# An attention and channel-mix kernel: loads of S and k spread over two DMA queues, output stored by 32-partition groups, fewer products on a zeroed tile

## The chip, the cores and the metric

The kernel runs on one core of one Trainium2 chip. A core has five engines that run their own instruction streams and meet at semaphores: PE (TensorE: products, with the weight loads listed apart as PEld), DVE (VectorE), ACT (ScalarE), POOL (GpSimd) and SP (SyncE). SP and ACT also issue DMAs; each has a queue of its own in the profile, SPq and ACTq. The metric is device microseconds of one execution.

## The reference

Two stages. The first is linear attention with a feature map that multiplies two sketches of a vector by each other; the second is a channel mix with a token shift.

```python
# q, k, v: (4 batches, 4 heads, 1088 tokens, 32), S1, S2: (8, 32)
def phi(x):
    a = einsum('rd,bhsd->bhsr', S1, x)
    b = einsum('rd,bhsd->bhsr', S2, x)
    return einsum('bhsi,bhsj->bhsij', a, b).reshape(..., 64)
q_p, k_p = phi(q), phi(k)
kv = einsum('bhsf,bhsd->bhfd', k_p, v)
z = sum(k_p, axis=2)
x = (q_p @ kv) / (q_p @ z + 1e-6)          # then heads side by side: (4, 1088, 128)

x_prev = x shifted by one token (a zero first)
xk = mu_k * x + (1 - mu_k) * x_prev
xr = mu_r * x + (1 - mu_r) * x_prev
out = sigmoid(xr @ w_r) * (relu(xk @ w_k) ** 2 @ w_v)     # w_k: 128 x 1024, w_v: 1024 x 128
```

## The kernel before

A batch has 1088 tokens, held as 34 blocks of 32: partition p of a tile stands for one of 32 token groups (of one head, or of all), and the 34 places within a group lie along the row. Each batch goes through three stages.

`stage_k` (from line 288) transposes k in two halves (kT, L296), multiplies by the masked sketch `Skb` (L303), transposes the result back (abT, L310), forms the 64 features (phk, L317) and accumulates kv with v (L326). The result `w` is masked on DVE (L336) and copied by two DMAs with its partition halves swapped (`ws`, L337).

`stage_q` transposes q (qT, L350), expands the features with `WS` (L362, copies on ACT at L374, products on DVE at L379), multiplies by w (L393) and divides by the denominator (L410 to L445). Its result is xT.

`stage_m` does the channel mix in three chunks of token blocks, `CH`: 12, 12 and 10 blocks of 32 tokens. Of a chunk it forms xk (L469), multiplies by w_k in eight products (L490), applies relu (kr, L495 on ACT or L497 on DVE), squares (the tile k2, named k in the profile: L499 on DVE or L501 on ACT), multiplies by w_v (L519), and by w_r for the gate (L514, sigmoid sg at L526); DVE forms the output tile `o` (L528), which has 128 tokens-of-a-product as partitions and three products side by side. SP stores o (L532). A product covers four blocks of 32 tokens; `first` names the column at which each of the three products begins. In a chunk of 10 blocks the third begins at column 192, so it overlaps the second, and only two of its blocks are stored. Store number i writes m blocks of product i, with a pattern whose outer count is m (4, or 2), then 32 token groups, then 128 values of four bytes; the rows in memory are 512 bytes long.

The order of the work on all engines is written out by hand: every operation has a number, and the string `ORDER` (L85 to L123) names them one after the other; "*5" behind a number puts five products on a zeroed tile (`stir`, L538, recorded as L540) ahead of it. Each engine works strictly through its own part of this order. The operation numbered 0 is the first `stir`, with 24 products. Ahead of it stand the loads that are issued in the code's own order: S1 and S2 on ACT's queue (L169, L170; both go into the tile Sst, which DVE transposes into St at L234, and from which Skb and WS come), then the two halves of the first k and the four parts of the first v on SP's (L181, L189), and the first q on ACT's (L202). All other loads are in `ORDER`, on SP. The chunks of the four batches are interleaved in it, so the last chunks to be computed are not the last in the code.

A DMA signals its completion on one of eight semaphores, taken in turn by all DMAs of both queues; in the orders below they read DMAHW0 to DMAHW7. A DMA waits, where its row says so, for the one before it on the same semaphore.

Of the kernel before, what the change touches and what calls it, by code (L numbers as in the profile page):

```python
# [17 lines left out]
def _ap(ap, new_ap, off=0):  # L18
    return dataclasses.replace(ap, ap=new_ap, offset=ap.offset + off)
# [13 lines left out]
class _Plan:  # L33
# [7 lines left out]
    def op(self, eng, cost, name, fn, need=(), uses=(), mode=None, kb=None, after=0.0, alt=(), stir=None):  # L41
        need = [n for n in need if n is not None]
        after = max([after] + [n["at"] for n in need if "at" in n])
        o = {"ways": [(eng, cost, fn)] + list(alt), "name": name, "need": [n for n in need if "at" not in n],
             "uses": list(uses), "mode": mode, "kb": kb, "after": after, "n": len(self.ops), "stir": stir}
        self.ops.append(o)
        return o
# [18 lines left out]
def kernel(  # L66
# [14 lines left out]
    nc = tc.nc  # L81
    B, H, S, D = q.shape
    R = S1.shape[0]
    DM, FF = moe_w_k.shape
    P = 128  # L85
    NFF = FF // P
    NB = S // 32
# [52 lines left out]
    op = plan.op  # L140

    def sb(tag, shape, dtype=F32, bufs=2):
        return _Buf(work, tag, bufs, shape, dtype)
# [3 lines left out]
    def ps(shape=(P, 512)):  # L147

        pair = shape[1:] == [KP, 512] and KP == 2
        t = _Buf(psum, None, 1, list(shape), F32)  # L150
        t.kind = "pair" if pair else "bank"
        banks.append(t)
        return t

    def dve(n, rate=0.96e3):
        return n / rate + 0.067
# [8 lines left out]
    Sst = const.tile([P, 2, D], F32)  # L165
    idle = const.tile([P, 512], BF16)
    nc.vector.memset(idle[:], 0.0)  # L167
    rows = [[D, R], [1, D]]
    nc.scalar.dma_start(Sst[:, 0, :], _ap(S1, [[0, 16]] + rows))  # L169
    nc.scalar.dma_start(Sst[:, 1, :], _ap(S2, [[0, 16]] + rows))  # L170

    kin = [const.tile([P, NB, D], F32, name=f"kin{b}") for b in range(3)]
# [2 lines left out]
    qTs = [const.tile([P, NB, 32], F32, name=f"qT{i}") for i in range(2)]  # L175
    LKB = NB * D * P * 4 / 1024

    def load_k(b, cuts):
        src = k[b].rearrange("h (sp t) d -> (h sp) t d", sp=32)
        for lo, hi in zip(cuts, cuts[1:]):  # L180
            nc.sync.dma_start(kin[b % 3][:, lo:hi, :], src[:, lo:hi, :])  # L181

    def load_q(b):
        nc.sync.dma_start(qin[b % 3][:], q[b].rearrange("h (sp t) d -> (h sp) t d", sp=32))
# [11 lines left out]
    wk = const.tile([DM, FF], BF16)  # L196
    wv = const.tile([P, NFF, DM], BF16)

    load_k(0, [0, NB // 2, NB])
    for g in range(4):  # L200
        load_v(0, g, nc.sync)
    nc.scalar.dma_start(qin[0][:], q[0].rearrange("h (sp t) d -> (h sp) t d", sp=32))  # L202
# [14 lines left out]
    for u in range(2):  # L217
        for p in range(2):
            lo = 32 + R * (2 * p + u)
# [36 lines left out]
    def arrival(nm, b):  # L256
        if (nm, b) not in IN:
            t = ARRIVE[nm][b]
            need = done[nm, b - 3] if b > 2 else []
            if nm == "k":  # L260
                IN[nm, b] = op("SP", 0.55, f"k{b}", lambda: load_k(b, [0, NB]), need, kb=LKB, after=t)
            elif nm == "q":
                IN[nm, b] = op("SP", 0.55, f"q{b}", lambda: load_q(b), need, kb=LKB, after=t)
            else:
                IN[nm, b] = [op("SP", 0.6, f"v{b}", lambda g=g: load_v(b, g, nc.sync), need, kb=LKB / 4, after=t)
                             for g in range(4)]
        return IN[nm, b] if isinstance(IN[nm, b], list) else [IN[nm, b]]
# [188 lines left out]
    def stage_m(b, xT, xo):  # L456
# [5 lines left out]
        order = (1, 2, 0)  # L462
        for j, ci in enumerate(order):
            c0, n = CH[ci]
# [7 lines left out]
            lo, hi = (0, 13) if ci == 0 else (c0 + 1, c0 + n + 1)  # L472
# [5 lines left out]
        for j, ci in enumerate(order):  # L478
            c0, n = CH[ci]
            k2 = sb("k2", [P, NFF, 12 * 32], BF16, 3)  # L480
            ok = []
            for cc in range(NFF // 2):
                kr = sb("kr", [P, 2, 12 * 32], BF16, 6)
                o2 = []
                for i0 in range(0, 2, KP):
                    kp = ps([P, KP, 512])

                    def up(kp=kp, c=2 * cc + i0, c0=c0, n=n):
                        for i in range(KP):
# [4 lines left out]
                            stir=lambda n, kp=kp: stir(kp[:, 0, :], n))  # L494
# [10 lines left out]
            o = sb("o", [P, 3, P], F32, 4)  # L505
            nt = (n + 3) // 4

            first = [128 * i if 4 * i + 4 <= n else 32 * n - P for i in range(nt)]

            def gate(rg=rg, c0=c0, first=first):  # L510
                for i, t in enumerate(first):
# [5 lines left out]
            def down(i, rd=rd, k2=k2, first=first):  # L517
                for c in range(NFF):
# [4 lines left out]
                    stir=lambda n, rg=rg: stir(rg.t.rearrange("p i m -> p (i m)"), n))  # L523
# [3 lines left out]
                sg[:, :nt, :], rg[:, :nt, :], ACTF.Sigmoid), [og], [rg, sg])  # L527
            oo = [op("DVE", dve(nt * P), f"o{b}.{ci}", lambda nt=nt, rd=rd, sg=sg, o=o: nc.vector.tensor_mul(  # L528
                o[:, :nt, :], rd[:, :nt, :], sg[:, :nt, :]), [os_] + od, [rd, sg, o])]
            def store(i, m, c0=c0, o=o, first=first):  # L530
                t = c0 + first[i] // 32 + 4 - m
                nc.sync.dma_start(_ap(out[b], [[DM, m], [NB * DM, 32], [1, DM]], t * DM), o[P - 32 * m:, i, :])  # L532

            for i in range(nt):
                m = min(4, n - 4 * i)
                op("SP", 0.55, f"out{b}.{ci}", lambda i=i, m=m, store=store: store(i, m), oo, [o], kb=16 * m)

    def stir(t, n):  # L538
        for _ in range(n):
            nc.tensor.matmul(t[:, :], idle[:, :P], idle[:], start=True, stop=True, skip_group_check=True)  # L540

    spare = ps()
    op("PE", 5.4, "stir", lambda: stir(spare, 24), [], [spare], mode="128x128")
    for b in range(B):
        stage_m(b, *stage_q(b, *stage_k(b)))
    for t, i in zip(banks, BANKS):
# [32 lines left out]
```

## Time and profile before

| | |
|---|---|
| time, three runs | 103.86 us median (103.39 to 104.56) |
| profiled execution, span from the first to the last instruction | 101.1 us |
| time of a run above that span | 2.3 to 3.5 us (the page gives the profiled execution by its span alone) |
| mean granted TensorE clock | 0.980 |
| busy: PE, DVE, ACT, POOL | 88.2, 82.5, 67.9, 17.1 us |
| DMA | 10.53 MB, mean 104 GB/s |
| stores of the output | 32 of 64 KB and 4 of 32 KB, all on SP |
| first loads of k | 2 of 272 KB; of S1 and S2 16 KB each |

A row of the chain or of the timeline begins with its start and its duration in microseconds; "L532" is the line of the kernel, a name before "<-" is what an instruction writes, and a bracket at the end tells how long the engine stood idle before it and what released it. PE's busy time holds the products on the zeroed tile too. In the list of waits stand the total, the count and the longest. A DMA's row shows the time in which its queue issues it, not its transfer; the transfer shows in the DMA share and in GB/s of a stretch.

### The profile page before, as it was taken

The page shows a single profiled execution, that of the slowest core. Times are in us where ns is not written, and L with a number is a line of the kernel's source. Part 1 is how long each engine was busy: PE and PEld are TensorE (multiplying, and loading weights), DVE is VectorE, ACT ScalarE, POOL GpSimd, SP SyncE. Part 2 cuts the span into 40 slices and gives each one's busy share as a digit, 9 for nine tenths or more (in the row PEclk, how much of TensorE's full clock was granted, in tenths as well). Part 3 has the DMA queues.
Part 4 walks back from the last instruction along what each step waited for, and adds up shares of the span by engine and source line. Part 5 has one row for each costly group of instructions (what it writes and reads, how often), then busy time and mean ns, then how long its engine had stood idle before and what let it go on. Part 6 is the DMA issues. An engine that isn't in the chain of part 4 may idle for free.

```text
span 101.1 us, 3298 instructions
## 1 busy us (share of the span) xinstructions
PE 88.2 (87%) x1328; PEld 54.6 (54%) x1328; DVE 82.5 (82%) x187; ACT 67.9 (67%) x172; POOL 17.1 (17%) x45
## 2 busy tenths in 40 slices
PE   5999999799999999899998999999979999996000
PEld 2343366243475356543555786586847887895000
DVE  1046989889999999899979999999999999994000
ACT  0500360452729999798996999999997999991000
POOL 6840000053000230000298300000180000000000
PEclk9999999999999999999999999999999999999965
DMA  2899999369300593018000010200210222322220
GB/s 46 256 283 212 319 247 312 76 184 302 122 12 0 136 323 134 6 26 215 12 0 0 6 26 1 82 14 13 84 58 7 74 71 78 87 82 87 83 75 13
DMA packets 10647, 10.53 MB, mean 104 GB/s; under 512 B 1288, under 2 KB 9352, under 8 KB 10632
## 3 DMA queue, kind: packets, MB, share of 16 engines
q1 hardware_dynamic: 10200, 9.74, 34.3%
q10 hardware_dynamic: 432, 0.59, 2.1%
q8 instruction: 10, 0.16, 0.7%
q14 instruction: 5, 0.04, 0.1%
HBM read 7.83 MB, written 2.23 MB: 100 GB/s over the span
## 4 chain that ended last, share of the span: by engine, by line
PE 42%; DVE 23%; DMA 13%; ACT 10%; issue 3%; ACTq 1%; SPq 0%; DVEq 0%
PE bank L519 12%; PE bank L490 10%; DMA kin<-in_k_dram 8%; ACT kr L495 7%; DVE phk L317 6%; DMA Sst<-in_S_dram 5%; DVE phq L379 5%; PE bank L410 3%; PE bank L362 3%; PE bank L514 3%; DVE k L499 3%; DVE xT L445 3%; PE bank L393 3%; PE bank L303 2%; PE bank L326 2%
## 5 line engine op out<-in xcount | busy, mean ns | idle before, releaser
L495 ACT ACTIVATE kr<-bank 128x384 bf16<-128x384 f32 (+1 forms) x89 | 35.7, 530 | 2.3 <-PE bank L490 2.0
L490 PE MATMUL bank<-xk,wk 128*128 128x384 bf16 (+1 forms) x96 | 22.9, 318 | 0.1
L519 PE MATMUL bank<-wv,k 128*128 128x128 bf16 x288 | 20.8, 219 | 0.6 <-DVE k L499 0.6
L374 ACT COPY a_sb<-bank 128x288 f32<-128x288 f32 (+1 forms) x32 | 10.1, 397 | 15.9 <-PE bank L362 15.9
L519 PEld LDWEIGHTS <-k 128*128 128x128 bf16 x288 | 18.2, 98 | 4.2 <-DVE k L499 1.1
L499 DVE TENSOR_TENSOR k<-kr 128x768 bf16<-128x768 bf16 (+1 forms) x34 | 17.7, 552 | 0.1
L476 POOL CAST xb<-xT 128x416 bf16<-128x416 f32 (+2 forms) x12 | 8.8, 758 | 42.1 <-DVE xT L451 26.4
L540 PE MATMUL bank<-idle 128*128 128x512 bf16 x40 | 11.5, 434 | 1.8 <-DVE idle L167 1.2
L362 PE MATMUL bank<-qT,WS 32*64 32x288 f32 (+1 forms) x256 | 12.2, 413 | 0.3 <-DVE w L336 0.2
L317 DVE TENSOR_TENSOR phk<-abT 128x768 f32<-128x768 f32 x12 | 12.3, 1035 | 0.0
L379 DVE TENSOR_TENSOR phq<-bank,a_sb 128x288 f32<-128x288 f32 (+1 forms) x32 | 12.1, 421 | 0.0
L501 ACT ACTIVATE k<-kr 128x768 bf16<-128x768 bf16 (+1 forms) x14 | 11.6, 844 | 0.1
L326 PE MATMUL bank<-vt,phk 128*64 128x64 f32 x288 | 10.6, 225 | 1.1 <-issue 0.5
L490 PEld LDWEIGHTS <-wk 128*128 128x128 bf16 x96 | 7.9, 97 | 6.5 <-issue 4.7
L326 PEld LDWEIGHTS bank<-vt,phk 128*64 128x64 f32 x288 | 9.2, 138 | 4.1 <-DVE phk L317 1.8
L540 PEld LDWEIGHTS <-idle 128*128 128x128 bf16 x40 | 4.0, 109 | 8.8 <-issue 3.7
L528 DVE TENSOR_TENSOR o<-bank,sg 128x384 f32<-128x384 f32 x12 | 6.6, 549 | 1.1 <-PE bank L519 1.1
L362 PEld LDWEIGHTS bank<-qT,WS 32*64 32x64 f32 x256 | 4.6, 129 | 4.8 <-issue 1.6
L469 DVE SCALAR_TENSOR_TENSOR xk<-xT,mu,uk 128x384 bf16<-128x384 f32 (+1 forms) x12 | 6.9, 579 | 0.0
L445 DVE TENSOR_TENSOR xT<-num,bank 128x256 f32<-128x256 f32 (+1 forms) x16 | 6.2, 425 | 0.5 <-PE bank L436 0.5
L465 ACT ACTIVATE uk<-xT,omu 128x384 f32<-128x384 f32 (+1 forms) x8 | 4.7, 602 | 2.7 <-DVE xT L445 2.7
L526 ACT ACTIVATE sg<-bank 128x384 f32<-128x384 f32 x12 | 6.3, 541 | 0.3 <-PE bank L514 0.3
(56 smaller groups left out, 94.0 us busy)
## 6 DMA issues: line engine op xcount, KB each, us to landing
out_dram<-o SPq DMA_DIRECT2D x32, 64.0 KB
vt<-in_v_dram SPq DMA_DIRECT2D x12, 144.0 KB
qin<-in_q_dram SPq DMA_DIRECT2D x3, 544.0 KB
kin<-in_k_dram SPq DMA_DIRECT2D x3, 544.0 KB
kin<-in_k_dram SPq DMA_DIRECT2D x2, 272.0 KB
qin<-in_q_dram ACTq DMA_DIRECT2D x1, 544.0 KB
wk_f<-in_moe_w_k_dram SPq DMA_DIRECT2D x1, 512.0 KB
wv_f<-in_moe_w_v_dram SPq DMA_DIRECT2D x1, 512.0 KB
```

The costliest lines, as they stand in the source:

```text
L317: nc.vector.tensor_mul(phk[:, lo:hi].rearrange("p t h j i -> p (t h) j i"), a_bc, b_bc)
L326: nc.tensor.matmul(kv[64 * u:64 * u + 64, p, :], phk[:, t, h, :, :].rearrange("p j i -> p (j i)"), _ap(vt[:, h, t, :], [pv, [(H - h) * NT ...
L362: nc.tensor.matmul(px[x][p][z][64 * v_:64 * v_ + 64, :n * 32], WS[32 * h:32 * h + 32, x, :], fl(qT[32 * h:32 * h + 32], t, t + n), start=T ...
L374: copy(a_sb[:, :n * 32], pa[:, :n * 32])
L379: lambda p=p, t=t, pb=px[1][p][z], a_sb=a_sb, n=n: nc.vector.tensor_mul(fl(phq[:, p], t, t + n), pb[:, :n * 32], a_sb[:, :n * 32]),
L445: xo[g] = op("DVE", dve(n * 32), f"x{b}", lambda g=g, t=t, n=n, lo=lo: nc.vector.tensor_mul(fl(xT, 1 + t, 1 + t + n), fl(num, t, t + n), p ...
L490: nc.tensor.matmul(kp[:, i, :n * 32], wk[:, (c + i) * P:(c + i + 1) * P], fl(xk, c0, c0 + n), start=True, stop=True)
L495: o2.append(op("ACT", act(n * 32 * KP), f"kr{b}.{ci}", lambda kp=kp, kr=kr, i0=i0, n=n: nc.scalar.activation(kr[:, i0:i0 + KP, :n * 32], k ...
L499: ok.append(op("DVE", dve(n * 64, 1.92e3), f"k2{b}.{ci}", lambda k2=k2, kr=kr, cc=cc, n=n: nc.vector.tensor_mul(k2[:, 2 * cc:2 * cc + 2, : ...
L501: alt=[("ACT", act(n * 64) + 0.1, lambda k2=k2, kr=kr, cc=cc, n=n: nc.scalar.activation(k2[:, 2 * cc:2 * cc + 2, :n * 32], kr[:, :, :n * 3 ...
L519: nc.tensor.matmul(rd[:, i, :], k2[:, c, first[i]:first[i] + P], wv[:, c, :], start=(c == 0), stop=(c == NFF - 1))
L540: nc.tensor.matmul(t[:, :], idle[:, :P], idle[:], start=True, stop=True, skip_group_check=True)
```

## The change

S1 is issued on SP's queue and S2 on ACT's, each as the first DMA of its queue. The two halves of the first k follow, one on each queue. In the channel mix, the three products of a chunk of 10 blocks begin at columns 0, 96 and 192, and the output tile is stored by groups of 32 partitions: store m takes partitions 32m to 32m + 31 of all three products (48 KB), for m = 0 to 3; in a chunk of 10 blocks the fourth takes only the third product's (16 KB). There are three store operations a chunk as before; the third issues two stores. For the chunk that comes last in the code, stores 1 and 3 are issued on ACT's queue. The first `stir` has 12 products.

```diff
-    nc.scalar.dma_start(Sst[:, 0, :], _ap(S1, [[0, 16]] + rows))
+    nc.sync.dma_start(Sst[:, 0, :], _ap(S1, [[0, 16]] + rows))
     nc.scalar.dma_start(Sst[:, 1, :], _ap(S2, [[0, 16]] + rows))
...
-    def load_k(b, cuts):
+    def load_k(b, cuts, queues=(nc.sync,)):
         src = k[b].rearrange("h (sp t) d -> (h sp) t d", sp=32)
-        for lo, hi in zip(cuts, cuts[1:]):
-            nc.sync.dma_start(kin[b % 3][:, lo:hi, :], src[:, lo:hi, :])
+        for lo, hi, queue in zip(cuts, cuts[1:], queues):
+            queue.dma_start(kin[b % 3][:, lo:hi, :], src[:, lo:hi, :])
...
-    load_k(0, [0, NB // 2, NB])
+    load_k(0, [0, NB // 2, NB], (nc.sync, nc.scalar))
...
-            first = [128 * i if 4 * i + 4 <= n else 32 * n - P for i in range(nt)]
+            step = (n - 4) // (nt - 1)
+            assert step * (nt - 1) == n - 4 and step in (3, 4)
+            first = [32 * step * i for i in range(nt)]
...
-            def store(i, m, c0=c0, o=o, first=first):
-                t = c0 + first[i] // 32 + 4 - m
-                nc.sync.dma_start(_ap(out[b], [[DM, m], [NB * DM, 32], [1, DM]], t * DM), o[P - 32 * m:, i, :])
-
-            for i in range(nt):
-                m = min(4, n - 4 * i)
-                op("SP", 0.55, f"out{b}.{ci}", lambda i=i, m=m, store=store: store(i, m), oo, [o], kb=16 * m)
+            def store(m, c0=c0, n=n, o=o, step=step, nt=nt, queue=nc.sync):
+                i = nt - 1 if step < 4 and m == 3 else 0
+                queue.dma_start(_ap(out[b], [[NB * DM, 32], [step * DM, nt - i], [1, DM]], (c0 + step * i + m) * DM),
+                                o[32 * m:32 * m + 32, i:, :])
+
+            end = b == B - 1 and j == len(order) - 1
+            for i, ms in enumerate(((0,), (1,), (2, 3))):
+                op("SP", 0.55 * len(ms), f"out{b}.{ci}", lambda ms=ms, store=store, end=end: [store(
+                    m, queue=nc.scalar if end and m % 2 else nc.sync) for m in ms], oo, [o], kb=48 * len(ms))
...
-    op("PE", 5.4, "stir", lambda: stir(spare, 24), [], [spare], mode="128x128")
+    op("PE", 5.4, "stir", lambda: stir(spare, 12), [], [spare], mode="128x128")
```

Three places of the order. The head of SP's part, before the change: the first k (kin0) and v (vt0), then the second batch's q and k (qin1, kin1), each waiting for an earlier DMA on its semaphore.

```order
L181 DMA kin0_69<-in_k_dram 128x544 x2
L189 DMA vt0_75<-in_v_dram 32x4x288 x3
L189 DMA vt0_75<-in_v_dram 32x4x224 [waits DMAHW0_49]
L251 DMA mu_80<-in_moe_mu_r_dram 128x1 [waits DMAHW1_49]
L184 DMA qin1_73<-in_q_dram 128x1088 [waits DMAHW2_49]
L181 DMA kin1_70<-in_k_dram 128x1088 [waits DMAHW3_49]
```

The same place after the change; the other half of kin0 now stands on ACT behind S2.

```order
L169 DMA Sst_64<-in_S1_dram 128x1x32
L181 DMA kin0_69<-in_k_dram 128x544
L189 DMA vt0_75<-in_v_dram 32x4x288 x3
L189 DMA vt0_75<-in_v_dram 32x4x224 [waits DMAHW0_49]
L251 DMA mu_80<-in_moe_mu_r_dram 128x1 [waits DMAHW1_49]
L184 DMA qin1_73<-in_q_dram 128x1088 [waits DMAHW2_49]
L181 DMA kin1_70<-in_k_dram 128x1088 [waits DMAHW3_49]
```

S1 has moved to the front of SP and one half of k away; the waits read alike, but the third semaphore, for which the second batch's q waits, was S2's and is now that of a half of k.

ACT's part near the end, before the change: the relu of the last chunk, a chunk of 10 blocks (320 columns), its square k2, and its sigmoid sg.

```order
L495 ACTIVATE kr_1759<-bank6_1757 128x384 [waits DVE_49,PE_49]
L495 ACTIVATE kr_1777<-bank2_1761 128x320 [waits DVE_49,PE_49]
L495 ACTIVATE kr_1709<-bank7_1774 128x320 [waits PE_49]
L495 ACTIVATE kr_1784<-bank4_1779 128x320 [waits PE_49,Activation_49]
L495 ACTIVATE kr_1798<-bank5_1752 128x320 [waits DVE_49]
L495 ACTIVATE kr_1784<-bank6_1786 128x320 [waits PE_49]
L495 ACTIVATE kr_1798<-bank2_1817 128x320 [waits PE_49]
L495 ACTIVATE kr_1777<-bank7_1815 128x320
L501 ACTIVATE k2_1820<-kr_1709 128x2x320 [waits Activation_49]
L526 ACTIVATE sg_1881<-bank2_1850 128x384 [waits PE_49]
```

The same place after it.

```order
L495 ACTIVATE kr_1754<-bank6_1752 128x384 [waits DVE_49,PE_49]
L495 ACTIVATE kr_1772<-bank2_1756 128x320 [waits DVE_49,PE_49]
L534 DMA out_0_dram<-o_1750 32x3x128 [waits DMAHW0_49,DVE_49]
L495 ACTIVATE kr_1703<-bank7_1769 128x320 [waits PE_49]
L495 ACTIVATE kr_1779<-bank4_1774 128x320 [waits PE_49,Activation_49]
L495 ACTIVATE kr_1793<-bank5_1747 128x320 [waits DVE_49]
L534 DMA out_0_dram<-o_1750 32x3x128 [waits DMAHW3_49]
L495 ACTIVATE kr_1779<-bank6_1781 128x320 [waits PE_49]
L495 ACTIVATE kr_1793<-bank2_1815 128x320 [waits PE_49]
L495 ACTIVATE kr_1772<-bank7_1813 128x320
L501 ACTIVATE k2_1818<-kr_1703 128x2x320 [waits Activation_49]
L528 ACTIVATE sg_1880<-bank2_1848 128x384 [waits PE_49]
```

Two stores of the output tile o_1750 stand among the relu of a chunk that is computed later.

The end of SP's part before the change, the stores of the last three output tiles.

```order
L532 DMA out_0_dram<-o_1810 4x32x128 [waits DMAHW3_49,DVE_49]
L532 DMA out_0_dram<-o_1810 2x32x128 [waits DMAHW4_49]
L532 DMA out_0_dram<-o_1810 4x32x128 [waits DMAHW5_49]
L532 DMA out_0_dram<-o_1859 4x32x128 [waits DMAHW6_49,DVE_49]
L532 DMA out_0_dram<-o_1859 4x32x128 [waits DMAHW7_49]
L532 DMA out_0_dram<-o_1859 4x32x128 [waits DMAHW0_49]
L532 DMA out_0_dram<-o_1891 4x32x128 [waits DMAHW1_49,DVE_49]
L532 DMA out_0_dram<-o_1891 4x32x128 [waits DMAHW2_49]
L532 DMA out_0_dram<-o_1891 2x32x128 [waits DMAHW3_49]
```

The same three tiles after it.

```order
L534 DMA out_0_dram<-o_1807 32x3x128 [waits DMAHW4_49,DVE_49]
L534 DMA out_0_dram<-o_1807 32x3x128 [waits DMAHW5_49]
L534 DMA out_0_dram<-o_1807 32x128 [waits DMAHW6_49]
L534 DMA out_0_dram<-o_1807 32x3x128 [waits DMAHW7_49]
L534 DMA out_0_dram<-o_1857 32x3x128 [waits DMAHW0_49,DVE_49]
L534 DMA out_0_dram<-o_1857 32x3x128 [waits DMAHW1_49]
L534 DMA out_0_dram<-o_1857 32x3x128 [waits DMAHW2_49]
L534 DMA out_0_dram<-o_1857 32x3x128 [waits DMAHW3_49]
L534 DMA out_0_dram<-o_1890 32x3x128 [waits DMAHW4_49,DVE_49]
L534 DMA out_0_dram<-o_1890 32x3x128 [waits DMAHW5_49]
L534 DMA out_0_dram<-o_1890 32x3x128 [waits DMAHW6_49]
L534 DMA out_0_dram<-o_1890 32x128 [waits DMAHW7_49]
```

Nine stores have become twelve, all of them on SP; the tile names count instructions and so differ.

## The prediction

> **What bounds the kernel now.** I read the page's slices first, then the chain that ended last, then SP's own waits and its queue in order of time, then the stretches around the end.
>
> ```profile
> DVE  1046989889999999899979999999999999994000
> DMA  2899999369300593018000010200210222322220
> GB/s 46 256 283 212 319 247 312 76 184 302 122 12 0 136 323 134 6 26 215 12 0 0 6 26 1 82 14 13 84 58 7 74 71 78 87 82 87 83 75 13
> ```
>
> A slice is 2.53 us. DVE is full from slice 4 to slice 37, so the middle is bound by compute. Two stretches are not: the first 15 us, where the DMA row is full, and the last three slices, where no engine computes and DMA is at two tenths. The chain says the same of its two ends:
>
> ```profile
> 1.38 4.82 DMA Sst<-in_S_dram
> 6.22 0.35 SPq L184
> 6.61 8.27 DMA kin<-in_k_dram
> ...
> 91.21 1.35 PE bank L519 x24
> ...
> 92.65 0.56 DVE o L528
> ```
>
> The last computed value is there at 92.65 + 0.56 = 93.21, yet the span is 101.1: 7.9 us, 8%, lie behind the last compute instruction. What fills them stands in SP's waits and in its queue (start, duration, line):
>
> ```profile
> SPq L574 <- DMA out_dram<-o: 3.9, 1, 3.9
> SPq L189 <- DMA qin<-in_q_dram: 2.7, 1, 2.7
> ...
> 61.88 0.68 SPq L532 DMA_DIRECT2D out_dram<-o  x1
> ...
> 82.25 0.55 SPq L532 DMA_DIRECT2D out_dram<-o  x1
> ...
> 87.58 0.54 SPq L532 DMA_DIRECT2D out_dram<-o  x1
> 88.17 0.54 SPq L532 DMA_DIRECT2D out_dram<-o  x1
> ...
> 94.76 0.69 SPq L532 DMA_DIRECT2D out_dram<-o  x1
> 95.49 0.65 SPq L532 DMA_DIRECT2D out_dram<-o  x1
> ```
>
> The last store is issued until 95.49 + 0.65 = 96.14, then SP waits 3.9 us for stores to land: 100.04. The remaining 1.1 us to 101.1 is the closing exchange between engines and stays. Two stores in a row stand 88.17 - 87.58 = 0.59 us apart, call it 0.58 (0.54 and a gap of 0.04). The stretches (length; busy times and counts of PE, PEld, DVE, ACT, POOL; PEclk; DMA share; GB/s) show why the landing takes 3.9:
>
> ```profile
> 63.00:63.25 0.25, 0.25 (x16) 0.00 (x0) 0.25 (x2) 0.25 (x2) 0.00 (x0) 1.00 0.07 16
> ...
> 97.00:98.00 1.00, 0.00 (x0) 0.00 (x0) 0.00 (x0) 0.00 (x0) 0.00 (x0) 0.51 0.27 81
> 98.00:98.50 0.50, 0.00 (x0) 0.00 (x0) 0.00 (x0) 0.00 (x0) 0.00 (x0) 0.50 0.14 43
> 99.50:99.75 0.25, 0.00 (x0) 0.00 (x0) 0.00 (x0) 0.00 (x0) 0.00 (x0) 0.50 0.05 14
> ```
>
> Share 0.27 of 16 engines is 4.3 engines; then, while the last store (2 x 32 x 128) is alone, 0.14 is 2.2 engines at half the rate. The stores' leading counts are 4 and 2. So a store of 64 KB drains on about four DMA engines at 81 GB/s, 0.79 us, and SP issues one each 0.58 us: a backlog grows that still drains 3.5 us after the last issue.
>
> **The change part by part. Stores.** The new ones have 32 partitions as leading count in both patterns. The nearest rows are the exchange of w (64 partitions by 512 B lines, 32 KB) and the loads of v (32 partitions):
>
> ```profile
> 58.24 1.11 SPq L337 DMA_DIRECT2D ws<-w  x2
> 60.00:60.25 0.25, 0.25 (x9) 0.25 (x7) 0.25 (x2) 0.25 (x2) 0.00 (x0) 1.00 0.60 125
> ...
> 44.30 0.58 SPq L189 DMA_DIRECT2D vt<-in_v_dram  x1
> 44.93 0.43 SPq L189 DMA_DIRECT2D vt<-in_v_dram  x1
> 46.00:46.25 0.25, 0.25 (x14) 0.00 (x0) 0.25 (x1) 0.25 (x2) 0.00 (x0) 1.00 1.04 364
> ```
>
> The second exchange of w moves 125 x 0.25 = 31 KB within a quarter of a microsecond at share 0.60: its bytes are not held to four engines. A store of 48 KB at that rate takes 0.39 us, less than the 0.58 between issues, so the backlog of transfers goes and what bounds the end is SP's issuing. That gets longer: four stores a chunk, not three.
>
> The two-queue end does not do what its words say. It is put on the chunk that the source writes last (batch 3, third in the chunk list), but the order table runs another chunk behind it: in the order of the changed kernel the two ACT stores (of o_1750) stand between ACT's kr, and three chunks' stores, 12 of them, follow on SP alone. So I count on SP. The chunk third from the end has its o from this row, the next two from the rows behind it:
>
> ```profile
> 89.33 0.55 DVE L528 TENSOR_TENSOR o<-bank,sg 128x384 f32<-128x384 f32 x1
> 91.00 0.55 DVE L528 TENSOR_TENSOR o<-bank,sg 128x384 f32<-128x384 f32 x1
> ```
>
> Its o is there at 89.88. SP, with four stores from 87.58 on, is free at 87.58 + 4 x 0.58 = 89.90. From there 12 stores without a gap: the last starts at 89.92 + 11 x 0.58 = 96.30, 0.8 later than the 95.49 of before. The last four start at 94.56, after their o (93.21), so nothing waits for compute. Then landing: from issue to first bytes 63.13 - 61.88 = 1.25 (the middle of the stretch in which they start); moving at most 0.3; last bytes to the end of the wait 100.04 - 99.63 = 0.4 (again the middle). That is 96.30 + 1.95 = 98.25 against 100.04: **-1.8 us**. The bounds are the spacing of issues: 0.47 as for v (0.43 and the gap) puts the last start at 89.92 + 11 x 0.47 = 95.1 and gives -3.0; 0.72 (0.69 + 0.03, the row at 94.76) puts it at 97.84 and gives -0.25. I take 0.58, since the ws rows with the same 512 B lines have 0.57 (1.11 for two, each about 0.54). The 12 more issues earlier in the kernel lie on a queue that waits for DVE anyway, and the loads are past by then.
>
> **Two stores on ACT.** Each is an issue on the queue of an engine that is busy until 91:
>
> ```profile
> 0.72 0.63 ACTq L169 DMA_DIRECT2D Sst<-in_S_dram  x1
> 90.23 0.74 ACT L501 ACTIVATE k<-kr 128x640 bf16<-128x640 bf16 x1
> ...
> L495 ACT ACTIVATE kr<-bank 128x384 bf16<-128x384 f32 (+1 forms) x89 | 35.7, 530 | 2.3 <-PE bank L490 2.0
> ```
>
> SP stores that chunk from 87.58 on, so its o is there by then; ACT comes to the first of the two with six kr (35.7 / 89 = 0.40 each) still ahead of the k at 90.23, at about 87.8. So it is the issue alone: 2 x (0.63 + 0.03) = 1.3 at most, 0 if ACT has enough in flight. Queued behind are those six kr and the k; DVE's last three squares wait for those kr, and both for the last products of L519 that start at 91.21. So compute ends up to 1.3 later. It is hidden in part: the last four stores start at 94.56 by the count above, 1.35 after their o; but the second last o also slips, from 91.55 to 92.85, and its stores would have started at 92.24. Cost 0 to 0.65 us; I take **+0.3**, the middle: of a kr's 0.53 us 0.13 lie beside its neighbour, so part of an issue is covered, and no row shows how much.
>
> **S first, k halves behind.** Now S1 and S2 are issued side by side at 0.72 and k's halves at about 1.4, instead of k at 0.72. S2, which landed at 6.20 behind k's and v's bytes, lands earlier, and DVE, whose St waits for it until 6.20, begins earlier. But DVE works in a fixed order:
>
> ```profile
> 9.80 0.33 SPq L189 DMA_DIRECT2D vt<-in_v_dram  x1
> ...
> 7.00 1.36 DVE L296 STREAM_TRANSPOSE kT<-kin 128x544 f32<-128x544 f32 x2
> 10.07 0.73 DVE L350 STREAM_TRANSPOSE qT<-qin 128x576 f32<-128x576 f32 x1
> 14.90 0.74 DVE L296 STREAM_TRANSPOSE kT<-kin 128x544 f32<-128x544 f32 x1 [0.33 <-DMA kin<-in_k_dram]
> ```
>
> qT needs q, which landed at 9.80 (SP's L189 waited its 2.7 us for it), 0.27 before DVE got there; and the next batch's kT waits for its k until 14.90. DVE time gained before 7 us turns into idle before 14.90 unless that k lands earlier, and it lands at the end of a stream that fills the DMA engines. So the gain is what moves that stream: later by one issue, 0.63 + 0.03 = +0.66, if k's bytes lead it; earlier by the hole that it has now:
>
> ```profile
> 4.00:4.50 0.50, 0.50 (x2) 0.15 (x1) 0.00 (x0) 0.16 (x1) 0.49 (x2) 1.00 0.40 105
> 4.50:5.00 0.50, 0.50 (x3) 0.23 (x2) 0.00 (x0) 0.00 (x0) 0.44 (x3) 1.00 0.81 166
> 5.00:5.50 0.50, 0.50 (x4) 0.22 (x3) 0.00 (x0) 0.00 (x0) 0.43 (x2) 1.00 0.63 207
> ```
>
> Here, with S2 under way, 0.5 x (0.60 + 0.19 + 0.37) = 0.58 us of the engines' time are lost. I take half of the hole, **-0.3**, nearer to the hole since with S landed first nothing of S lies among k, v and q; ends -0.58 and +0.66.
>
> **12 products fewer.** At nothing: the loads for the 24 run until 7.82 (below), and the first products on k are loaded at 8.41 after 0.59 us of waiting for kT. If kT comes earlier, 24 products would be in the way, so this keeps the way free; its risk is a rival below. The shifted product columns of the 10-block chunks (0, 96, 192 for 0, 128, 192) are as many products: nothing.
>
> Sum: -1.8 + 0.3 - 0.3 = -1.8 on the profiled execution, 101.1 to 99.3. The median of the runs, 103.86, stands 2.76 above that span, the fastest 2.3; 103.86 - 1.8 = **102.1**.
>
> **The rivals.** *Issuing eats it.* If a store to sixteen engines costs the 0.72 of the last rows, the end gains 0.25 only: -0.25 + 0.3 - 0.3, 103.6, no change. For it: the rows of 0.65 to 0.69; against: they occur only in the backlog. 0.10.
>
> *The whole chain moves up.* If q and the next k come forward too, DVE's first kT sets the shift: k's 544 KB, issued at 1.4, flow from 2.65 on at the second slice's 256 GB/s until 4.8, kT starts at 5.0 and not 7.0, and 103.86 - 1.5 - 2.0 = 100.4. Against it: the full DMA row. 0.08.
>
> *PE slows down between its products.* The loads of the zeroed tile show two rates:
>
> ```profile
> 4.56 0.15 PEld L540 LDWEIGHTS <-idle 128*128 128x128 bf16 x1 [0.27 <-issue]
> 4.92 2.90 PEld L540 LDWEIGHTS <-idle 128*128 128x128 bf16 x14 [0.21 <-issue]
> 8.41 0.64 PEld L303 LDWEIGHTS bank<-kT,Skb 128*32 128x32 f32 x16 [0.59 <-DVE kT L296]
> ```
>
> Until 4.92, 3.75 us after the first product, one comes each 0.43 us, afterwards each 0.21. Twelve end at about 5.5, and PE then idles until kT, 2.9 us if that stays at 8.4. Should the slow rate come back for another 3.75 us, PE does 1.9 us less work of what DVE's rows at 15 to 17 wait for, DVE has 0.33 of slack: 1.6 late, net -0.2, 103.7. No row here shows the slow rate again after such a gap. [...] 0.06, a sixth of it slower still.
>
> *Stores from a quarter of the partitions are slow.* If the rate went with the partitions, 32 would give half of w's 125, 62 GB/s. The last 26 stores (24 of 48 KB, 2 of 16) are 1184 KB from 82.25 + 1.25 = 83.5 on: 19.1 us, to 102.6, end of the wait 103.0, 3.0 later than now: 103.86 + 3.0 - 0.3 = 106.6, slower. It decides below 1184 / 17.5 = 68 GB/s, where the wait ends 1.34 later and outweighs the start's gain by 1%. Against it: 364 GB/s at 46.0, when two loads into 32 partitions each can have been moving, so 180 for one. [...] 0.04.
>
> **How the numbers follow.** The forecast's case gets the remaining 0.72; its sum lies between -3.0 - 0.58 = -3.6 and about -0.25 + 0.65 + 0.66, whose part above -1.04 holds a tenth of it. About 1%, 1.04 us, is what a measurement of this kernel tells from no change. Faster: 0.65 of the 0.72 and the chain's 0.08, 0.73. Within 1%: the other 0.07, issuing 0.10, PE 0.05, 0.22. Slower: 0.04 and 0.01, 0.05. The range runs from 100.5, near the low bound of 100.3 and the chain's 100.4, to 103.4, which leaves out issuing, PE and the slow stores, 0.20.
>
> **What would show it.** In the changed profile: stores 0.55 to 0.6 apart on SP, without a gap over the last 12; a DMA share in bursts above 0.4 instead of a flat 0.28 from 86 on; a final wait of about 1.4 to 2 us instead of 3.9; two issues on ACT near 88 with kr behind them; St before 4, kT before 7, and the idle before the second kT at 14.9 grown to 1 us or more. I am wrong if the flat share stays, if SP's spacing passes 0.7, or if the second kT moves by more than a microsecond.

## The result: faster by 4.4%, more than forecast

| | before | after |
|---|---|---|
| time, median (runs beside each other) | 103.62 us (103.21 to 104.56) | 98.36 us (98.08 to 98.65) |
| ratio | | 0.956 (95% interval 0.950 to 0.963) |
| span of the profiled execution | 101.1 us | 96.0 us |
| end of the last output tile `o` | 93.21 us | 91.51 us |
| from there to the end of the span | 7.89 us | 4.49 us |

The forecast was 102.1 us with a range down to 100.5. The sign was right, the size was not: 5.1 us of the span went, not 1.8. The table puts 1.7 of them ahead of the last `o` and 3.4 behind it. First the slices of the profile after (2.40 us each):

```profile
DVE  1268979979999999999979999999999999999510
DMA  0999999299200396006200001220230133424442
GB/s 5 253 344 266 363 262 314 58 259 295 68 10 0 85 310 230 0 21 175 71 0 7 0 7 27 62 55 0 62 82 0 27 85 83 108 53 105 89 103 48
```

DVE is at six tenths in the third slice, where it was at four, and the stretch without compute at the end is not quite two slices long, where it was three of 2.53 us. Behind the last `o` and just ahead of it (SP's queue, SP's waits, then two stretches with length, busy times, clock, DMA share and GB/s):

```profile
85.88 1.12 SPq L534 DMA_DIRECT2D out_dram<-o  x1
...
90.83 3.26 SPq L534 DMA_DIRECT2D out_dram<-o  x7
...
93.66 0.43 SPq L534 DMA_DIRECT2D out_dram<-o  x1
SPq L578 <- DMA out_dram<-o: 0.7, 2, 0.4
...
91.75:92.00 0.25, 0.00 (x0) 0.00 (x0) 0.00 (x0) 0.00 (x0) 0.00 (x0) 1.00 0.71 160
92.00:92.25 0.25, 0.00 (x0) 0.00 (x0) 0.00 (x0) 0.00 (x0) 0.00 (x0) 1.00 0.22 45
```

Seven stores take 3.26 us, 0.47 each, where the old ones stood 0.58 apart. The share swings between 0.71 and 0.22 instead of lying flat at 0.27: a store's bytes are gone before the next store's come, so nothing piles up, and SP's last wait is 0.7, not 3.9. The new stores use more engines: 0.71 of 16 is 11 on average within that quarter of a microsecond. The old stores, with outer counts of 4 and 2, had shares of 0.27 and 0.14, which is 4.3 and 2.2 engines; the new ones, with an outer count of 32, 0.71 and 11 in that stretch. The updates of the stores' semaphores in the trace differ too: an old store of 64 KB gets one about 1 us after its issue begins and four more 2.3 us or more after it (two more for 32 KB), a new one gets sixteen, most of them within 0.2 us.

The start, on DVE and PE, and the head of the chain that ended last:

```profile
3.27 0.24 DVE L234 STREAM_TRANSPOSE St<-Sst 128x64 f32<-128x64 f32 x1 [2.15 <-DMA Sst<-in_S_dram]
5.10 1.62 DVE L296 STREAM_TRANSPOSE kT<-kin 128x544 f32<-128x544 f32 x2 [1.06 <-DMA kin<-in_k_dram]
13.84 0.74 DVE L296 STREAM_TRANSPOSE kT<-kin 128x544 f32<-128x544 f32 x1 [0.66 <-DMA kin<-in_k_dram]
6.78 1.18 PE L303 MATMUL bank<-kT,Skb 128*32 128x288 f32 x16 [1.42 <-DVE kT L296]
...
1.47 4.49 DMA kin<-in_k_dram
...
5.98 7.84 DMA kin<-in_k_dram
```

S is no longer in the chain: it begins with the first k, which releases the second batch's k on SP at 5.98. The first kT starts at 5.10 (7.00 before), the first products on k at 6.78 (8.42), and the second batch's kT at 13.84 (14.90), still waiting for its k.

### The profile page after: what moved, and what is told of

Read it like the earlier page. It is cut to its first block, busy times and chain, and to the rows that moved or that the text cites. A ratio compares the mean times of both kernels' runs of the same rounds, so it can differ in the third digit from the quotient of the medians.

```text
span 96.0 us, 3286 instructions
## 1 busy us (share of the span) xinstructions
PE 85.3 (89%) x1316; PEld 53.3 (55%) x1316; DVE 82.7 (86%) x187; ACT 68.0 (71%) x172; POOL 17.1 (18%) x45
## 4 chain that ended last, share of the span: by engine, by line
PE 36%; DVE 31%; DMA 13%; ACT 10%; issue 4%; SPq 1%; DVEq 0%; ACTq 0%
DMA kin<-in_k_dram 13%; PE bank L521 12%; PE bank L490 9%; DVE phk L317 8%; ACT kr L495 7%; DVE phq L379 5%; DVE k L499 4%; DVE xT L445 4%; PE bank L362 3%; PE bank L516 3%; PE bank L303 3%; DVE xk L469 2%; PE bank L410 2%; ACT a_sb L374 2%; DVE o L530 2%
## 5 line engine op out<-in xcount | busy, mean ns | idle before, releaser
L544 PE MATMUL bank<-idle 128*128 128x512 bf16 x28 | 8.5, 442 | 1.8 <-DVE idle L167 1.2
L296 DVE STREAM_TRANSPOSE kT<-kin 128x544 f32<-128x544 f32 x8 | 5.8, 731 | 1.8 <-DMA kin<-in_k_dram 1.7
L544 PEld LDWEIGHTS <-idle 128*128 128x128 bf16 x28 | 2.6, 109 | 7.1 <-issue 3.2
(56 smaller groups left out, 94.9 us busy)
```

## The experiments

Thirteen runs. "Theory" in the expectations means the reading that was open at that moment. The times of before beside them were 102.55 to 102.89 us in the median, so ratios are compared, each against the runs of before on the same chip.

### Each half of the change alone

New stores only, with the old loads and 24 products (against the changed kernel; the shifted product columns and the two stores on ACT stay in):

```diff
-    nc.sync.dma_start(Sst[:, 0, :], _ap(S1, [[0, 16]] + rows))
+    nc.scalar.dma_start(Sst[:, 0, :], _ap(S1, [[0, 16]] + rows))
...
-    load_k(0, [0, NB // 2, NB], (nc.sync, nc.scalar))
+    load_k(0, [0, NB // 2, NB], (nc.sync, nc.sync))
...
-    op("PE", 5.4, "stir", lambda: stir(spare, 12), [], [spare], mode="128x128")
+    op("PE", 5.4, "stir", lambda: stir(spare, 24), [], [spare], mode="128x128")
```

> The new stores alone, with the old start (S1, S2 on ACT, both halves of k on SP, 24 products). Theory A (two separate gains): the end between the last o and the end of the span shrinks from 7.9 to 4.5 us and nothing else moves: 3.4 us faster than before, 100.2. Theory B (the stores do it all, also what lies ahead of them): the full 5.2 us, 98.4. Theory C (the prediction's sum for the stores): 1.5 faster, 102.1.

Measured: 98.61 us (98.06 to 99.37), ratio 0.965 (0.958 to 0.973).

New loads and 12 products only, with the old stores (against the kernel before; `load_k` takes the queues as in the change):

```diff
-    nc.scalar.dma_start(Sst[:, 0, :], _ap(S1, [[0, 16]] + rows))
+    nc.sync.dma_start(Sst[:, 0, :], _ap(S1, [[0, 16]] + rows))
...
-    load_k(0, [0, NB // 2, NB])
+    load_k(0, [0, NB // 2, NB], (nc.sync, nc.scalar))
...
-    op("PE", 5.4, "stir", lambda: stir(spare, 24), [], [spare], mode="128x128")
+    op("PE", 5.4, "stir", lambda: stir(spare, 12), [], [spare], mode="128x128")
```

> The new start and 12 products alone, with the old stores. Theory A: the last o comes 1.7 us earlier and the old end of 7.9 us follows: 101.9. Theory B: no change, 103.6. Theory D (the old stores are held back by transfers, so that part of an earlier start is lost in the backlog): 0.5 to 1 faster, 102.6 to 103.1. Theory C (the prediction): 0.3 faster.

Measured: 100.92 us (100.70 to 101.20), ratio 0.988 (0.982 to 0.994).

The product of the two ratios is 0.953, which lies in the interval of the whole change: the two halves add, and neither hides the other. The stores are the larger, 3.5% of about 102.5, 3.5 us; the start brings 1.3 us. Lines of the run with the new stores alone (SP's last wait, a stretch, DVE), and below them SP's last wait with the old stores behind the new start:

```profile
SPq L578 <- DMA out_dram<-o: 0.7, 2, 0.4
...
4.00:4.50 0.50, 0.50 (x2) 0.15 (x1) 0.00 (x0) 0.16 (x1) 0.49 (x2) 1.00 0.86 231
...
5.59 0.24 DVE L234 STREAM_TRANSPOSE St<-Sst 128x64 f32<-128x64 f32 x1 [4.48 <-DMA Sst<-in_S_dram]
14.43 0.74 DVE L296 STREAM_TRANSPOSE kT<-kin 128x544 f32<-128x544 f32 x1
```

```profile
SPq L574 <- DMA out_dram<-o: 3.9, 1, 3.9
```

The 3.9 us at the end belong to the old stores, whatever the start. And with the old start, the hole in the DMA stream at 4.0 us, on which the prediction priced the start, isn't there: share 0.86, against 0.40 in the profile of before.

### The start's two parts against each other

The changed kernel with 24 products, and with the old loads (12 products):

```diff
-    op("PE", 5.4, "stir", lambda: stir(spare, 12), ...)
+    op("PE", 5.4, "stir", lambda: stir(spare, 24), ...)
```

> The changed kernel with 24 products again. If the removal does nothing (the prediction): 98.4. If 24 products are in the way of the earlier kT (they end at 8.3, the first products on k could start at 6.8): the second kT is reached at about 14.6 instead of 13.84, 0.7 to 0.8 slower, 99.1.

Measured: 98.40 us (98.19 to 98.75), ratio 0.963 (0.956 to 0.970).

```diff
-    nc.sync.dma_start(Sst[:, 0, :], ...)
+    nc.scalar.dma_start(Sst[:, 0, :], ...)
-    load_k(0, [0, NB // 2, NB], (nc.sync, nc.scalar))
+    load_k(0, [0, NB // 2, NB], (nc.sync, nc.sync))
```

> The new stores and 12 products with the old order of the first loads. Theory A: as the stores alone, 100.2, since with S landing at 6.2 nothing on k can start before 7; if the idle PE gets slow in the gap it is slower than the stores alone by up to 1.6 us, 101.8. Theory B: 98.4.

Measured: 100.43 us (100.01 to 100.88), ratio 0.983 (0.976 to 0.989).

Neither part shows a gain alone. Beside the new stores alone (0.965), S first with 24 products gives 0.963, no difference that these intervals can show: PE works on the zeroed tile until 8.57, and the first products on k wait behind it until 8.50, 0.39 later than with the new stores alone (8.11). Twelve products with S late cost 1.8%. Why stands in that run's PE rows and stretches (the column after the five busy times is the granted TensorE clock):

```profile
8.79 1.77 PE L303 MATMUL bank<-kT,Skb 128*32 128x288 f32 x16 [2.58 <-DVE kT L296]
10.49 2.30 PE L544 MATMUL bank<-idle 128*128 128x512 bf16 x5
...
8.50:9.00 0.50, 0.21 (x4) 0.16 (x8) 0.24 (x1) 0.00 (x0) 0.00 (x0) 1.00 1.09 292
9.00:9.50 0.50, 0.50 (x12) 0.27 (x8) 0.00 (x0) 0.00 (x0) 0.00 (x0) 0.73 1.10 280
9.50:10.00 0.50, 0.50 (x12) 0.07 (x4) 0.35 (x1) 0.00 (x0) 0.00 (x0) 0.50 1.06 246
```

PE stood idle for 2.58 us, from 6.21 on; the granted clock went to half at about 9.2 (0.73 is the mean of the half microsecond from 9.0 on), three microseconds after the last product and 0.4 after PE had begun again, and the 16 products took 1.77, not 1.18. This is the rival "PE slows down between its products", to which the prediction gave 0.06; it becomes real when S is late, and S first is what keeps it away in the changed kernel (idle 1.42, products 1.18). A gap of 2.58 us sufficed here. From the last product to the half clock it is not the same time everywhere: 2.7 us with k on SP and 3.1 with q ahead (both below), and at the end of the span 2.0 in after (90.86 to 92.84) and 4.5 in before (92.55 to 97.01).

### What in the loads' order brings it: k's queue or q's place

Both halves of k on SP, S first as in the change; on ACT's queue q then stands right behind S2:

```diff
-    load_k(0, [0, NB // 2, NB], (nc.sync, nc.scalar))
+    load_k(0, [0, NB // 2, NB], (nc.sync, nc.sync))
```

> The changed kernel with both halves of k on SP's queue behind S's first half, and nothing but S's second half ahead of the rest on ACT's; all else as after. Theory A (what the loads' order brought is S being there early: the first St at 3.27 and no gap ahead of the first kT's product; which queue carries k's halves does not matter): the first kT stays within 0.5 us of 5.10, the second kT within 0.5 us of 13.8, and the time within 0.5 us of after's. Theory B (the split of k over both queues brings the second kT forward): the second kT, which waits for k, falls back by about 1 us towards before's 14.90; with SP's queue bounding the end as in the run with 24 products, about half of it shows, some 0.5 us slower than after.

Measured: 101.09 us (100.43 to 102.06), ratio 0.988 (0.983 to 0.992), 3.5% above after on the same chip (97.69, below). Neither theory had this size. Two things had moved: k's second half had gone to SP, and q had been issued at 1.40, not at 2.03. The next run moves q alone:

```diff
+    nc.scalar.dma_start(qin[0][:], ...)
     load_k(0, [0, NB // 2, NB], (nc.sync, nc.scalar))
     for g in range(4):
         load_v(0, g, nc.sync)
-    nc.scalar.dma_start(qin[0][:], ...)
```

> The changed kernel with q's load on ACT's queue put ahead of the second half of k, which stays on ACT's queue; all else as after. With both halves of k on SP the first kT began at 8.07, but that run had also moved q forward by one issue, from 2.03 to 1.40. Theory A (two halves on one queue come one behind the other, and the first kT waits for the later one): with a queue each the first kT stays at 4.8 to 6 us and the time within 0.5 us of after's, 97.6 to 98.4. Theory B (q's 544 KB ahead of k's second half hold it back, whichever queue it is on): the first kT starts at 7 to 8.5, PE idles over 2 us ahead of its first product on k and its 16 products take about 1.8 to 2.2 and not 1.18, and the time is 2 to 3.5 us above after's.

Measured: 101.10 us (100.79 to 101.60), ratio 0.985 (0.978 to 0.992). The rows of both, k on SP first, q ahead below:

```profile
8.07 1.37 DVE L296 STREAM_TRANSPOSE kT<-kin 128x544 f32<-128x544 f32 x2 [4.03 <-DMA kin<-in_k_dram]
9.49 2.15 PE L303 MATMUL bank<-kT,Skb 128*32 128x288 f32 x16 [3.58 <-DVE kT L296]
```

```profile
1.41 0.59 ACTq L199 DMA_DIRECT2D qin<-in_q_dram  x1
2.03 0.45 ACTq L181 DMA_DIRECT2D kin<-in_k_dram  x1
...
7.95 1.37 DVE L296 STREAM_TRANSPOSE kT<-kin 128x544 f32<-128x544 f32 x2 [3.88 <-DMA kin<-in_k_dram]
9.38 2.13 PE L303 MATMUL bank<-kT,Skb 128*32 128x288 f32 x16 [3.05 <-DVE kT L296]
```

The starts of the first kT and of the products on k agree within 0.15 us, with k on one queue and on two. So it is q's place: 544 KB of q issued 0.6 us ahead of the second half of k, which DVE transposes first, hold the first kT back by 2.9 us, to 7.95, and the idle PE then comes under the half clock as well (granted clock 0.50 from about 9.5 on, and from about 8.6 on with k on SP; the 16 products take 2.1 us and not 1.18). With q ahead of it, the second half gains nothing from a queue of its own; what the second queue does in the change is to put that half ahead of q. Whether one queue with q behind both halves would do as well was not run.

### The kernel before, and after, once more

Both kernels without any edit: the one before once, the changed one twice.

> The kernel before once more, for a second profile of it. If the stretch without transfers at 4.0 to 5.5 us, and PE's pause of 0.49 us ahead of w's product at 41 us, belong to the kernel, both are here again. If they belonged to one execution, the second transpose of k starts near 14.4 without a wait for k, as in the run with the new stores alone, and w is ready 0.4 us earlier relative to it. The old stores are issued every 0.58 us either way, and the last one is issued about 4 us after the last o ends.

Measured: 103.39 us, span 101.4. A stretch of it, and the second batch's k on SP and on DVE:

```profile
4.00:4.50 0.50, 0.50 (x2) 0.15 (x1) 0.00 (x0) 0.16 (x1) 0.49 (x2) 1.00 0.91 205
...
5.73 0.59 SPq L181 DMA_DIRECT2D kin<-in_k_dram  x1
16.07 0.74 DVE L296 STREAM_TRANSPOSE kT<-kin 128x544 f32<-128x544 f32 x1 [0.34 <-DMA kin<-in_k_dram]
```

The hole at 4.0 us belonged to one execution; so did PE's pause of 0.49 us at 41 us, which is not here. But the expected second kT near 14.4 is wrong too: with the old start and 24 products it comes at 14.43, 14.90 or 16.07, from one execution to the next. Here k was issued earlier than in the first profile (5.73 against 6.61) and landed later. What stretched its transfer isn't settled.

> The changed kernel beside the next three. 0.956 of before again; the last o near 91.5, the last store issued near 93.7, the span near 96.2.

Measured: 97.59 us (97.36 to 97.87), ratio 0.950 (0.944 to 0.956); second kT at 13.77.

> The changed kernel beside the version with two chunks on two queues, on the same chip and with as many rounds: 97.6 to 98.4 us, SP's stores every 0.47 us, the last of them 1.8 to 2.2 us after the last o ends.

Measured: 97.69 us (96.97 to 98.45), ratio 0.954 (0.949 to 0.960); second kT at 13.04. With the new start and 12 products the second kT lies between 13.0 and 14.1 in all profiles but one, that of the run with two stores of the last chunk on ACT (15.65, an execution of 99.73 us).

### The end: how many stores SP issues last

All stores on SP; the two on ACT moved to the chunk that is computed last (out3.2 in the order); and the second and fourth stores of each of the two chunks 3.1 and 3.2 on ACT:

```diff
-            end = b == B - 1 and j == len(order) - 1
+            end = False                                # all on SP
...
+            end = b == B - 1 and j == 1                # the chunk computed last
...
+            end = b == B - 1 and j < 2                 # the last two chunks of the last batch
```

> All stores on SP, none on ACT. Theory I: 18 stores from 85.9 on, the last at 85.9 + 17 x 0.47 = 93.9, 0.2 slower than the changed kernel. If the two issues on ACT cost compute what the prediction set for them (0.3): 0.1 faster. If the collision with ACT costs nothing: 0.9 slower.

Measured: 98.52 us (98.47 to 98.86), ratio 0.959 (0.954 to 0.965), 0.9 us above after on the same chip (97.59).

> The stores 1 and 3 of the chunk that is computed last (batch 3, second in the chunk list) go to ACT's queue, instead of those of the chunk last in the code. Theory I (the end is set by SP's issuing: 16 stores in a row from 85.9 on at 0.47, after one that lasted 1.12 beside ACT's issue): without that collision the last store on SP starts at 85.9 + 15 x 0.47 = 93.0 instead of 93.7, 0.7 faster than the changed kernel. Theory II (the end is set by the last o and the landing): no difference.

Measured: 98.12 us (97.54 to 99.73), ratio 0.953 (0.944 to 0.962). No difference from after on the same chip (0.950) can be seen, and the interval is wide: it settles nothing. Its profile is that of the execution of 99.73 us, the longest of its four, and is not compared.

> Stores 1 and 3 of the last two computed chunks go to ACT's queue. Theory I: SP has 14 stores from 85.9 on, its last two right behind the last o, at 91.55 and 92.0: 1.6 faster than the changed kernel. Theory II: no difference. If the two issues ahead of the last sigmoid hold ACT up behind the second last o: up to 0.8 of it lost.

Measured: 97.19 us (96.57 to 97.77), ratio 0.948 (0.940 to 0.955).

> The version with the second and fourth stores of both chunks 3.1 and 3.2 on ACT's queue, and all of chunk 3.0 on SP's, timed more closely beside after on the same chip. Theory (the end is as long as SP's row of stores, 0.47 us each; two fewer there are worth up to 0.9 us until the last o itself sets the end): 0.4 to 0.9 us faster than after. Rival (ACT's own issues, 0.85 us each for two, hold back the last chunk by as much): within 0.3 us of after.

Measured: 97.11 us (96.89 to 97.75), ratio 0.951 (0.946 to 0.956), beside 97.69 for after. SP's last store with all on SP, and below, with two chunks on two queues, the last stores of SP and ACT and SP's waits:

```profile
94.30 0.42 SPq L534 DMA_DIRECT2D out_dram<-o  x1
```

```profile
92.18 0.43 SPq L534 DMA_DIRECT2D out_dram<-o  x1
89.82 0.85 ACTq L534 DMA_DIRECT2D out_dram<-o  x2
91.82 0.86 ACTq L534 DMA_DIRECT2D out_dram<-o  x2
SPq L578 <- DMA out_dram<-o: 1.3, 3, 0.8
```

Two stores more or fewer in SP's last row move the end by about 2 x 0.47: from the last `o` to the end of the span it is 4.85 us with all on SP, 4.1 to 4.5 in after (4.1 in two of its three profiles), 3.2 with two chunks split. Of the last 0.9 a third is given back, since the last `o` itself comes 0.2 to 0.3 later (table below). What is left, 0.4 and 0.6 us on two chips, points the same way twice, but the intervals overlap; this is the fastest version measured, not one shown to beat after.

### One table for all of it

Second kT: start of the transpose of the second batch's k. All from the profiled executions, one for each row.

| kernel | second kT | end of last `o` | between | span | behind last `o` |
|---|---|---|---|---|---|
| before | 14.90 | 93.21 | 78.3 | 101.1 | 7.9 |
| before again | 16.07 | 93.66 | 77.6 | 101.4 | 7.7 |
| new stores alone | 14.43 | 92.01 | 77.6 | 96.1 | 4.1 |
| new start and 12 alone | 13.69 | 91.27 | 77.6 | 98.7 | 7.4 |
| after | 13.84 | 91.51 | 77.7 | 96.0 | 4.5 |
| after again | 13.77 | 91.45 | 77.7 | 95.5 | 4.1 |
| after, third | 13.04 | 90.77 | 77.7 | 94.9 | 4.1 |
| after with 24 | 14.57 | 92.33 | 77.8 | 96.4 | 4.1 |
| after with old loads | 15.44 | 94.02 | 78.6 | 98.1 | 4.1 |
| k on SP | 16.54 | 95.60 | 79.1 | 99.7 | 4.1 |
| q ahead | 16.38 | 94.61 | 78.2 | 98.7 | 4.1 |
| all stores on SP | 14.05 | 91.75 | 77.7 | 96.6 | 4.9 |
| two chunks split | 13.33 | 91.34 | 78.0 | 94.5 | 3.2 |
| two chunks split, again | 13.85 | 91.79 | 77.9 | 95.0 | 3.2 |

The kernel is three pieces. Up to the second kT the loads decide, with the products in the way; from there to the last `o` it is 77.6 to 77.8 us, whatever start or stores, but for the first profile of before (PE's pause), the three runs with the half clock, and ACT's four stores; behind the last `o` the stores decide. The 4.5 of after goes with the long first issue of its row (1.12 at 85.88): the other profiles with the same stores have 4.1, and in two of them, k on SP and q ahead, the longest issue of the end is 0.69 and 0.53.

## Why the prediction was wrong, step by step

**Bound at the end: right.** SP's issues and the drain on four engines (share 0.27) filled the 7.9 us; with the old stores the final wait of 3.9 is there in all three profiles, with the new ones it is 0.7, and 1.3 with two chunks split. That the flat share goes was right as well.

**"I take 0.58, since the ws rows ... have 0.57": the mechanism right, the term mis-sized.** The spacing is 0.47, the lower bound that the loads of v gave. The prediction put the last store 3.09 us behind the last `o` (96.30 against 93.21); it starts 2.15 behind it (93.66 against 91.51), and 1.8 in the second profile of after (93.23 against 91.45). That is 0.9 to 1.3 us. The row on which the choice rested hides two sizes: of the two ws issues from 58.24 to 59.35 the first took 0.47 and the second 0.60, so a mean of 0.57 stood for neither. What makes an issue short: not the bytes, since most of the old stores took 0.54 each, of 64 KB and of 32 KB alike. The old stores' semaphores get five or three updates and the new ones' sixteen, but no run changes the number of engines by itself, and ws, which gets sixteen updates too, has 0.47 and 0.60. So the cause of the shorter issue stays open.

**"Landing 1.95", and 1.1 behind it: too long by 0.7 together.** From the start of the last issue to the end of the span it is 2.34 us (96.0 - 93.66), where the prediction had 1.95 + 1.1 = 3.05. It had read the 1.25 to first bytes from an old store; the page of after gives the whole landing of a new one:

```profile
out_dram<-o SPq DMA_DIRECT2D x42, 48.0 KB, 1.6
```

The last number is the microseconds from issue to landing. So half of the 0.7 is the landing, 1.6 and not 1.95, and half lies behind it, 2.34 - 1.6 = 0.74 and not 1.1.

**"Two stores on ACT, +0.3": zero.** ACT comes to them at 85.89 and 86.83, not near 87.8; 1.7 of that is the shift of the whole chain up to the last `o`:

```profile
85.89 0.38 ACTq L534 DMA_DIRECT2D out_dram<-o  x1
86.83 0.33 ACTq L534 DMA_DIRECT2D out_dram<-o  x1
```

The issues are 0.38 and 0.33, not 0.63, and the compute behind them isn't late: 77.7 us from the second kT to the last `o`, the same as with all stores on SP. That the two-queue end sits on a chunk with three more behind it was right; that it therefore gains nothing was not. It takes two stores out of SP's last row, and that row, not the last `o`, sets the end.

**"So the gain is what moves that stream ... I take half of the hole, -0.3": the step that failed by its mechanism.** Two things were wrong in it. The hole was one execution's, and neither the new stores alone nor the second profile of before has it. And the second kT, which waited only 0.33 us for its k, was taken as pinned by the transfers alone; but DVE's own work ahead of it, which the change does bring forward, set it nearly as well. That work is done at 13.18 in after (13.84 - 0.66), against 14.57 before (14.90 - 0.33) and 14.43 with the new stores alone, where kT starts without a wait. So the second kT could move up until it met k, and k landed earlier too, at 13.8 and not at 14.9. The prediction's own sign of being wrong came: the second kT moved by 1.06 us, and the idle time ahead of it grew to 0.66, not to 1 or more.

Why k lands earlier stays open. The prediction's chain has S2's landing at 6.20 as what let SP issue the second batch's q and k at 6.22 and 6.61, a release that the forecast left out; in after they are issued at 5.10 and 5.98. But an earlier issue is not an earlier landing. The second batch's k, its issue and its time to landing, with the new stores alone, and below with k on SP:

```profile
5.90 0.51 SPq L181 DMA_DIRECT2D kin<-in_k_dram  x1
kin<-in_k_dram SPq DMA_DIRECT2D x1, 544.0 KB, 8.5
```

```profile
6.84 0.33 SPq L181 DMA_DIRECT2D kin<-in_k_dram  x1
kin<-in_k_dram SPq DMA_DIRECT2D x1, 544.0 KB, 7.2
```

Issued 0.94 us later, it landed 0.4 earlier (14.0 against 14.4); and in the second profile of before, issued at 5.73, it landed at 16.0. What the whole start brought: 1.1 us at the second kT between the two first profiles, 1.7 at the last `o` (0.6 of that lies behind the second kT, in before's execution alone, PE's pause of 0.49 among it); 1.3 us by the runs of the start alone.

**"12 products fewer, at nothing": half right.** The cover named for the 24 was there, and removing them can gain only once kT comes early: 0.8 to 1.6 us at the last `o` on top of S first (92.33 with 24; 91.51, 91.45 and 90.77 with 12), and 0.7 to 1.4% by the ratios (0.963 against 0.956, 0.950 and 0.954), whose intervals overlap. The risk named for it, PE's slow rate after a gap, is real at 2.58 us of idleness and would have cost 1.8%; S first keeps the gap at 1.42.

**The other rivals.** Issuing at 0.72 did not happen: in after's last row the first issue took 1.12, the fifteen behind it 0.37 to 0.44. That a store goes to sixteen engines, as this rival says, no run shows: the share was 11 of 16 within a quarter of a microsecond. The stores from a quarter of the partitions are not slow: 160 GB/s in a quarter of a microsecond (91.75 to 92.00). The whole chain moving up, 100.4 us and 0.08, was right for the first kT (5.0 forecast, 5.10 measured), but of its 2.0 us 1.1 reached the second kT; the rest of the distance to 98.36 is the stores.

In sum, on the profiled executions: forecast -1.8; the row of issues 0.9 more, landing and closing 0.7 more, ACT 0.3 more, the start 1.4 more (0.6 of it that execution of before): -5.1, which is the span's 101.1 to 96.0. By the runs of each half alone the stores brought 3.5 where the sum had 1.5 (1.8 less ACT's 0.3), the start 1.3 where it had 0.3; so the mis-sized end is the larger part of the miss.

## What to carry to other kernels

A drain at the end is priced by the queue's issue spacing (0.58 us before, 0.47 after) times the stores left in its last row, and by the share of the DMA engines: give a store a pattern like the one that was spread here (outer count 32 and 11 engines within a quarter of a microsecond, against 4 and 4.3), and take stores off the row, even stores of an earlier chunk (0.9 us here, all on SP against after). A step that looks pinned by a landing load by 0.3 us has a second bound just behind: work out when the engine itself would be ready, and do not take the load's issue for its landing. A feature of one profile, such as a hole in a stream, needs a second execution before a term rests on it. When a row of products on a zeroed tile is cut, what follows has to come earlier by about as much, or PE stands idle (2.58 us with S late, and then 1.77 us for 16 products that take 1.18 otherwise); and a large load that nobody needs yet belongs behind the last piece of the one that is waited for (q ahead of k's second half held the first kT back by 2.9 us).

## What was not expected of the hardware

- A gap of 2.58 us without products was enough for the granted clock to go to half, and it did so about three microseconds after the last product, when PE was already at work again; after a gap of 1.42 us in the changed kernel it stayed whole.
- A load of 544 KB issued 0.6 to 0.9 us ahead of a load of 272 KB moved the landing of that one by about 2.9 us, on the same queue or on another.
- A load of 544 KB issued at 6.84 us landed before one issued at 5.90 in another run, 7.2 us against 8.5 after its issue.
- The same store is issued in 0.43 us in the middle of a row, but the first of the last row took 1.12 in one execution, with an issue on ACT beside it; the longest issue of the end was 0.69 with k on SP, 0.53 with q ahead, and 0.69 with no store on ACT.
